# Last block of a block-FFT convolution: products in place over the x spectra, one summing visit per third

## The chip, the cores and the metric

The kernel runs on one NeuronCore of one Trainium2 chip. Its engines run their own instruction streams in program order and meet through semaphores: TensorE (PE, matmuls into PSUM), VectorE (DVE), ScalarE (ACT), GpSimd (POOL) and SyncE (SP, which here only issues DMAs). The metric is the device time of one execution in microseconds (us); less is better. Kernels are compared by the median of several executions on the same chip.

## The reference

The output is the concatenation of two independent halves of 576 channels each, over S = 2048 positions. Half A is a sliding attention with 32 heads of 18 channels, a window of 8 positions at dilation 2, and two projections. Half B is a gated long convolution:

```python
def _B_ref(q, k, v, shift_k, ssm_k, ssm_D):
    ...
        k_shift = k_shift + k_pad[:, t:t + S, :] * shift_k[:, ks - 1 - t][None, None, :]
    kv = k_shift * v
    ...
    y_f = kv_f * kf_f[None, :, :, :]
    y = irfft(y_f)[:S]
    y = y + kv * ssm_D[None, None, :]
    return q * y
```

The change lies wholly in half B. What is computed is not altered by it.

## The kernel before

**The convolution by blocks.** The 2048 positions are cut into NBL = 4 blocks of 512. For each block i the spectrum of kv is made once and kept in the SBUF tile `xw` at `HB * XG[i]`, in three parts of HB = 2304 columns: two components and their sum. The filter's four block spectra lie in the tile `Ks` in the same manner. The spectrum of output block j is the sum over i = 0..j of (x spectrum i) times (filter spectrum j - i). The three parts let one complex product be made with three real ones. Each part's columns are worked on in three thirds t of QTR = 768 columns (192 channels by four frequency groups).

**Products (L1092 to L1101).** `products(j, t, i)` is one VectorE multiply of 128x2304 (three parts of 768 columns) of `xw` by `Ks`. The result goes to one of five homes: places in the tiles `av`, `v`, `qk` (two) and `Ks` that are free by then. Block 3 rotates over the first four of them, block 2 over all five. There are 30 products in the list `todo` (L1225), in the order j, t, i: numbers 0 to 2 for block 0, 3 to 8 for block 1, 9 to 17 for block 2, and 18 to 29 for block 3 (18 to 21 are third 0 with i = 0 to 3, 22 to 25 third 1, 26 to 29 third 2).

**Sums (L1105 to L1141).** `sums` adds a group of products into two PSUM accumulators `ps_z` (r = 0 and r = 1) by matmuls with plus or minus identity. TensorE works as four 64x64 tiles there, and one product is 16 matmuls, shown in the trace as four rows of four. After the last product of a third (i = j), ScalarE evicts r = 0 and then r = 1 to `av` (L1139); only the very last r = 1 goes over VectorE (L1137).

**The inverse transform (L1146 to L1222).** It is cut into units that TensorE does between the sums. For blocks 0 to 2 the 576 channels go in two halves a and b, each with three units, queued in the order a0, b0, a1, b1, a2, b2. Units 0 and 1 are eight 128x128 matmuls each (L1158) into the same PSUM tile: unit 0 starts it, ScalarE copies the result out (L1161), unit 1 accumulates on top of it, and ScalarE copies again. Unit 2 (`back`) is eight 64x64 matmuls (L1199) on the copies, evicted by ScalarE at L1206. Unit a0 or a1 needs only thirds 0 and 1 of its block, b0 or b1 thirds 1 and 2. Two such PSUM tiles (tag A) exist, so a and b have one each. Block 3 is different: after its third 1, units u0 and u1 (128x384) and a `back` are queued for the first 384 channels; the last 192 channels go through `last` (L1171) at the very end. After `back` of half b comes the gate: one VectorE multiply by q (L1212), three stores from SP (L1080, L1083) and, for blocks 0 and 1, the load of a later q by three DMAs on POOL (L1087, L1089).

**What sets the order.** The program's order is each engine's order. `groups` (L1229 to L1234) says which products are summed in one visit of TensorE. Block 0 has one product to a visit, block 1 two, block 2 three. Block 3 has pairs, and its last product, 29, is a visit of its own: 18,19 / 20,21 / 22,23 / 24,25 / 26,27 / 28 / 29. Ahead of a visit `sums` calls `until()` once, or twice for a group of more than two; each call takes the next number from the tuple `PLACES` (L19) and puts that many queued units ahead of the visit. The last seven numbers are 1, 2, 1, 4, 1, 1, 0. So the order on TensorE from the end of block 2's sums is: a0, sums 18 19, b0 a1, sums 20 21, b1, sums 22 23, a2 b2 (the queue is then empty), sums 24 25, u0, sums 26 27, u1, sums 28, sums 29, `back`, `last`.

The loop at L1253 emits products ahead of the visit that uses them, up to two past the group's last one, and one fewer at the group that ends with product 17 (L1254). Gates that are due are emitted ahead of the next product (L1242); the gate of block 2 is kept back until after product 29 (L1249).

Of the kernel before, what the change touches and what calls it, by code (L numbers as in the profile page):

```python
# [39 lines left out]
def view(t, offset, dims):  # L40

    return bass.AP(tensor=t.tensor, offset=t.offset + offset, ap=[list(t.ap[0])] + [list(d) for d in dims])
# [3 lines left out]
def kernel(  # L46
# [37 lines left out]
    NBL, BL = 4, 512  # L84
# [4 lines left out]
    HB = 4 * D  # L89
    QTR = 768  # L90
# [21 lines left out]
    xw = main.tile([128, 12 * HB], BF16, name="xw")  # L112
# [5 lines left out]
    XG = (9, 0, 3, 6)  # L118
# [52 lines left out]
    def k_at(m, part):  # L171
        return 3 * HB * (3 - m) + HB * part
# [139 lines left out]
    def dve(n, fn, ready=0.0, ns=0.53):  # L312

        fn()
        clk["D"] = max(clk["D"], ready) + n * ns / 1000 + 0.125
        return clk["D"]
# [23 lines left out]
    def need(label):  # L340
        while any(u[2] == label for u in units):
            pop()
# [369 lines left out]
    for i in range(NBL):  # L712
# [30 lines left out]
        for n, u in enumerate(mirrors):  # L743
            n = AT[n] if n < 2 else AT[i]
# [347 lines left out]
    def products(j, t, i):  # L1092

        homes = ((av, 0), (v, 6912), (qk, 9216), (qk, 9216 + HB), (Ks, k_at(3, 2)))
        n = npr[0]
        pr = view(*homes[(4, 1, 2, 3, 0)[(n - 9) % 5] if j == 2 else n % 4 if n < 9 else (n - 18) % 4], [[QTR, 3], [1, QTR]])
        npr[0] += 1
        r = dve(3 * QTR, lambda: nc.vector.tensor_tensor(  # L1098
            pr, view(xw, HB * XG[i] + QTR * t, [[HB, 3], [1, QTR]]),
            view(Ks, k_at(j - i, 0) + QTR * t, [[HB, 3], [1, QTR]]), ALU.mult))  # L1100
        return pr, r  # L1101
# [3 lines left out]
    def sums(j, t, group):  # L1105

        for _ in range(1 + (len(group) > 2)):
            until()
        for i, pr, ready in group:
            out = sum_of(j, t, i, pr, ready)  # L1110
        return out
# [113 lines left out]
    todo = [(j, t, i) for j in range(NBL) for t in range(3) for i in range(j + 1)]  # L1225
# [2 lines left out]
    clk["P"] = clk["D"]  # L1228
    groups = []  # L1229
    for n, (j, t, i) in enumerate(todo):  # L1230
        if (i if j == 2 else i % 2) and (j, t, i) != todo[-1]:
            groups[-1].append(n)
        else:
            groups.append([n])  # L1234
    prs, made_to = {}, 0

    def produce(n):
        if n < len(todo):
            j, t, last = todo[n]
            for i in range(last + 1):  # L1240
                need(f"fx{i}")
            due(1.0)  # L1242
            for new, tile_, at in ((last == 0, Ks, k_at(j, 0)), (last == j, xw, HB * XG[j])):
                if new and (j == 0 or t == 0) and (tile_ is xw, at) not in given:
                    at, w = (at + QTR * t, QTR) if j == 0 else (at, HB)
                    a, b, c = (view(tile_, at + HB * part, [[1, w]]) for part in range(3))
                    dve(w, lambda: nc.vector.tensor_tensor(c, a, b, ALU.add))
            prs[n] = products(*todo[n])
            if n == len(todo) - 1:  # L1249
                while late:  # L1250
                    late.popleft()[1]()

    for group in groups:  # L1253
        while made_to < min(group[-1] + 3 - (group[-1] == 17), len(todo)):  # L1254
            produce(made_to)
            made_to += 1
        j, t, i = todo[group[-1]]
        if (t, todo[group[0]][2]) == (0, 0):
            need(f"inv{j - 2}")
        r = sums(j, t, [(todo[n][2],) + prs.pop(n) for n in group])  # L1260
        new = []
        if i == j and t == 2 and j < NBL - 1:
            a, b = inverse(j, 0, HD, r), inverse(j, HD, HD, r)
            new = [a[0], b[0], a[1], b[1], a[2], b[2]]
        elif i == j and j == NBL - 1 and t > 0:
            new = inverse(j, 0, 2 * TH, r) if t == 1 else inverse(j, 2 * TH, TH, r)
        for u in new:
            units.insert(sum(w[2][:3] == "inv" for w in units), u)
# [35 lines left out]
```

## Time and profile before

| | |
|---|---|
| median of 3 runs | 214.94 us (214.34 to 215.21) |
| the profiled execution | 215.25 us |
| its span in the profile | 213.5 us |
| share of the chain that ended last | PE 51%, DVE 23%, DMA 9%, ACT 7%, issue 6% |
| granted TensorE clock over the span | 0.998 |

In the timeline, a row is a run of like instructions of one engine: its start and its duration in us, the engine, the line of the kernel, the operation, output and input, and how many. In brackets stands the idle time before it on its engine, and what ended that idle time. The rows of one engine can overlap a little, since its instructions are pipelined; start to start is then the better measure. Ahead of the stretch that the change touches lie the projections, the attention and the forward spectra (to about 152 us of the span); block 3's own sums run from 190.5 us to 205.9 us, and the end of the kernel is the inverse of block 3's last 192 channels, its gate and its stores.

### The profile page before, as it was taken

Reading aid. Unit: us, or ns where it says so; the run is one execution under the profiler, and the core shown is the slowest. Engines: PE = TensorE matmul, PEld = TensorE weight load, DVE = VectorE, ACT = ScalarE, POOL = GpSimd, SP = SyncE. Lnnn points to the kernel's source line nnn. Section 1 sums busy time; section 2 is a strip of 40 time slices with the busy share of each in tenths; the row PEclk is TensorE's granted clock in tenths of the full one; section 3 lists DMA queues with packets and bytes.
Section 4 is the critical chain, followed back from the end, with each engine's and each line's share of the span. In section 5 each row is a group of like instructions: output and inputs, shape, how many; then the busy total and the mean of one; then the engine's idle time right before and its main releaser. Section 6 shows DMA issues by size and latency. Waiting matters only on the chain.

```text
span 213.5 us, 5089 instructions
## 1 busy us (share of the span) xinstructions
PE 200.7 (94%) x2114; PEld 112.0 (52%) x2122; DVE 197.6 (93%) x150; ACT 150.8 (71%) x218; POOL 68.6 (32%) x104
## 2 busy tenths in 40 slices
PE   7999899999879999999999999998999999999891
PEld 3443344445545656453355456765566667666560
DVE  7989999999969999979999999979999999799972
ACT  4699764787897979975378568964578797756630
POOL 8999992102683255220190000004330001102000
PEclk9999999999999999999999999999999999999999
DMA  6999999999492655998999893957994105353033
GB/s 209 295 325 228 275 323 298 229 144 223 91 140 27 86 71 98 187 164 179 225 249 220 173 228 87 167 182 174 235 251 138 60 3 166 114 169 111 3 110 111
DMA packets 34084, 36.12 MB, mean 169 GB/s; under 512 B 17459, under 2 KB 28847, under 8 KB 34062
## 3 DMA queue, kind: packets, MB, share of 16 engines
q1 hardware_dynamic: 26380, 23.11, 44.7%
q0 software_dynamic: 5216, 10.19, 25.3%
q10 hardware_dynamic: 2466, 2.51, 3.4%
q8 instruction: 16, 0.26, 0.5%
q14 instruction: 6, 0.05, 0.1%
HBM read 13.11 MB, written 4.72 MB: 83 GB/s over the span
## 4 chain that ended last, share of the span: by engine, by line
PE 51%; DVE 23%; DMA 9%; ACT 7%; issue 6%; SPq 2%; DVEq 0%; ACTq 0%
DVE tB L560 9%; PE ps_z L1126 9%; DVE xw L564 8%; PE ps_inv L1158 7%; PE ps_wo L1020 6%; PE ps_proj L363 5%; PE ps_acc L964 4%; PE ps_fk L610 4%; PE ps_fx L766 4%; DMA TB<-av 4%; PE ps_log L837 3%; DMA xw<-in_A_wqkv_dram 3%; DMA kj<-in_B_k_dram 2%; DVE av L947 2%; ACT Ks L670 2%
## 5 line engine op out<-in xcount | busy, mean ns | idle before, releaser
L363 PE MATMUL ps_proj<-xw 128*128 128x512 bf16 x153 | 36.6, 380 | 1.3 <-issue 0.6
L822 DVE TENSOR_TENSOR av<-qk 128x4096 bf16<-128x4096 bf16 (+1 forms) x16 | 31.5, 2018 | 2.3 <-ACT xw L592 2.1
L363 PEld LDWEIGHTS <-xw 128*128 128x128 bf16 x160 | 14.3, 98 | 20.6 <-issue 5.9
L1098 DVE TENSOR_TENSOR qk<-xw,Ks 128x2304 bf16<-128x2304 bf16 x14 | 18.7, 1355 | 2.0 <-PE ps_z L1126 1.7
L1139 ACT ACTIVATE av<-ps_z 128x768 bf16<-128x768 f32 x23 | 17.4, 809 | 4.3 <-PE ps_z L1126 4.3
L397 ACT ACTIVATE qk<-ps_proj 128x1024 bf16<-128x1024 f32 x14 | 14.3, 1023 | 8.4 <-PE ps_proj L374 4.5
L768 ACT ACTIVATE xw<-ps_fx 128x576 bf16<-128x576 f32 x32 | 18.7, 669 | 1.1 <-PE ps_fx L766 1.1
L560 DVE TENSOR_TENSOR tB<-kj,skb 128x4608 bf16<-128x4608 bf16 (+1 forms) x8 | 19.3, 2416 | 0.1
L670 ACT ACTIVATE Ks<-ps_fk 128x576 bf16<-128x576 f32 x32 | 18.6, 687 | 1.2 <-PE ps_fk L611 1.2
L766 PE MATMUL ps_fx<-xw,TB 128*128 128x288 bf16 x128 | 18.0, 286 | 0.9 <-ACT xw L592 0.7
L1020 PE MATMUL ps_wo<-qk 128*128 128x288 bf16 x128 | 17.6, 287 | 0.0
L610 PE MATMUL ps_fk<-Ks,TB 128*128 128x384 bf16 x62 | 16.5, 326 | 1.0 <-ACT Ks L670 0.7
L964 PE MATMUL ps_acc<-av,ident 64*64 64x512 bf16 x160 | 15.7, 378 | 0.7 <-DVE av L947 0.7
L1158 PE MATMUL ps_inv<-av,TI 128*128 128x288 bf16 (+1 forms) x112 | 15.7, 292 | 0.6 <-ACT av L1139 0.6
L766 PEld LDWEIGHTS <-TB 128*128 128x128 bf16 x128 | 11.8, 97 | 7.3 <-issue 4.6
L397 ACT ACTIVATE v<-ps_proj 128x1024 bf16<-128x1024 f32 x9 | 9.4, 1039 | 8.8 <-PE ps_proj L374 4.5
L611 PE MATMUL ps_fk<-Ks,TB 128*128 128x192 bf16 x62 | 15.2, 245 | 0.0
L1087 POOL DMA_DIRECT2D TB<-in_B_q_dram x4 | 3.0, 738 | 37.8 <-DVE v L1098 23.8
L968 ACT ACTIVATE qk<-ps_acc 128x1024 bf16<-128x1024 f32 x8 | 8.2, 1024 | 9.7 <-PE ps_acc L964 9.7
L1020 PEld LDWEIGHTS <-qk 128*128 128x128 bf16 x128 | 11.7, 98 | 5.3 <-issue 2.5
L947 DVE TENSOR_TENSOR av<-Ks,v 128x4096 bf16<-128x4096 bf16 x6 | 13.7, 2286 | 0.8 <-PE ps_acc L964 0.8
L1161 ACT ACTIVATE v<-ps_inv 128x576 bf16<-128x576 f32 (+1 forms) x14 | 9.5, 677 | 6.4 <-PE ps_inv L1158 6.3
(194 smaller groups left out, 467.6 us busy)
## 6 DMA issues: line engine op xcount, KB each, us to landing
Ks<-Ks POOLq DMA_DIRECT2D x7, 576.0 KB, 8.7
TB<-av SPq DMA_DIRECT2D x12, 256.0 KB, 5.4
kj<-in_B_k_dram SPq DMA_DIRECT2D x6, 504.0 KB, 6.0
vt<-in_B_v_dram SPq DMA_DIRECT2D x8, 288.0 KB, 4.9
Ks<-av SPq DMA_DIRECT2D x8, 256.0 KB, 5.4
out_dram<-qk ACTq DMA_DIRECT2D x5, 288.0 KB, 4.0
Ks<-in_A_x_dram SPq DMA_DIRECT2D x2, 576.0 KB, 5.2
xw<-in_A_wqkv_dram SPq DMA_DIRECT2D x2, 576.0 KB, 5.9
```

The source lines that it names most:

```text
L363: nc.tensor.matmul(ps[:, jp, :], wq(kb, comp, 128 * ct, 128), xT(kb, 1024 * jj + 512 * jp, 512), **se)
L397: nc.scalar.activation(view(t, o + pad + 1024 * jj, [[512, 2], [1, 512]]), ps[:], ACT.Copy)
L560: dve(2304 * n, lambda: nc.vector.tensor_tensor(to, view(kj, row * D, [[D, n], [D, 4], [1, D]]), view(skb, row * D, [[D, n], [0, 4], [1, D ...
L610: nc.tensor.matmul(o[:, 0:2], w, rhs[:, 0:2], start=start, stop=stop)
L670: nc.scalar.activation(view(Ks, k_at(m, cs ^ (m & 1)) + 96 * gi, [[768, 3], [384, 2], [1, 96]]), acc3(ps), ACT.Copy, scale=(PSG, MSG)[cs][ ...
L766: nc.tensor.matmul(ps[:, pm, 0:HD], TX[:, 2 * pm + c, 128 * gi:128 * gi + 128], kv[:, 2 * c + pm, HD * h:HD * h + HD], start=(c == 0), sto ...
L768: nc.scalar.activation(view(xw, HB * XG[i] + 96 * gi + 1152 * h, [[HB, 2], [384, 3], [1, 96]]), view(ps, 0, [[512, 2], [96, 3], [1, 96]]), ...
L822: return P, at, step, dve(1024 * nj, lambda: nc.vector.tensor_tensor(view(P, at, [[step, 4], [256, nj], [1, 256]]), view(t, o + 256 * hh, ...
L964: nc.tensor.matmul(acc[64 * o:64 * o + 64, h, :], ident[64 * h:64 * h + 64, 64 * h:64 * h + 64], view(P, 256 * u, [[2048, 2], [1, 256]])[6 ...
L1020: nc.tensor.matmul(ps[:, r, 0:HD], oT(hh, j + 2 * r, t)[:, o:o + 128], wo[:, t // 2, t % 2, HD * h:HD * h + HD], start=(t == 0 and h == 0) ...
L1126: nc.tensor.matmul(view(acc[r], 512 * h, [[192, 2], [96, 2], [1, 96]])[o:o + 64], w[64 * h:64 * h + 64, 64 * h:64 * h + 64], pr[64 * h:64 ...
L1158: nc.tensor.matmul(ps[:, c, 0:n], TI[:, sl, pm, 128 * c:128 * c + 128], Yall[:, j % 2, pm, sl, c0:c0 + n], start=(pm == 0 and sl == 0), st ...
```

## The change

Three places are edited. Products of block 3 are written over the x spectrum that they are made from (each product of block 3 is the last reader of its slice of `xw`), so they use none of the homes. In `groups`, a visit of block 3 now holds a whole third, other than the very last product: 18 to 21, 22 to 25, 26 to 28, and 29. And the exception for the group that ends with product 17 is gone, so that products 18 and 19 are both emitted ahead of that group's sums. `PLACES` is as it was. Blocks 0 to 2 keep their homes and groups.

```diff
@@ products
         homes = ((av, 0), (v, 6912), (qk, 9216), (qk, 9216 + HB), (Ks, k_at(3, 2)))
         n = npr[0]
-        pr = view(*homes[(4, 1, 2, 3, 0)[(n - 9) % 5] if j == 2 else n % 4 if n < 9 else (n - 18) % 4], [[QTR, 3], [1, QTR]])
+        pr = view(*homes[(4, 1, 2, 3, 0)[(n - 9) % 5] if j == 2 else n % 4], [[QTR, 3], [1, QTR]]) if j < NBL - 1 else \
+            view(xw, HB * XG[i] + QTR * t, [[HB, 3], [1, QTR]])
         npr[0] += 1
@@ groups
-        if (i if j == 2 else i % 2) and (j, t, i) != todo[-1]:
+        if i and (j, t, i) != todo[-1]:
             groups[-1].append(n)
         else:
             groups.append([n])
@@ the loop over groups
-        while made_to < min(group[-1] + 3 - (group[-1] == 17), len(todo)):
+        while made_to < min(group[-1] + 3, len(todo)):
             produce(made_to)
             made_to += 1
```

## The prediction

> **What bounds it now.** First the page, for which engines are full:
>
> ```profile
> PE 200.7 (94%) x2114; PEld 112.0 (52%) x2122; DVE 197.6 (93%) x150; ACT 150.8 (71%) x218; POOL 68.6 (32%) x104
> ```
>
> TensorE and VectorE are both nearly full, so the averages decide nothing; what counts is which of them ends last where the change is. Next the chain of waits (start, length, engine, what), in the stretch of block 3:
>
> ```profile
> 198.31 1.19 ACT v L1206 x2
> 199.50 0.02 issue
> 199.52 0.82 ACT av L1139
> 200.34 0.04 issue
> 200.38 1.46 PE ps_inv L1158 x8
> 201.84 1.42 PE ps_z L1126 x32
> 203.27 1.41 PE ps_inv L1158 x8
> 204.67 1.45 PE ps_z L1126 x32
> ```
>
> The chain is TensorE's own work, with one stop at 199.5 to 200.4, where u0 waits for ScalarE to evict the sums of third 1. An eviction's end releases TensorE 0.04 us later (200.34 to 200.38). VectorE is not in it. Third, the timeline of TensorE, cut to the points where the kind of work changes:
>
> ```profile
> 189.16 0.33 PE L1126 MATMUL ps_z<-qk,identn 64*64 64x384 bf16 x4
> 189.43 1.15 PE L1158 MATMUL ps_inv<-av,TI 128*128 128x288 bf16 x8
> 190.51 0.36 PE L1126 MATMUL ps_z<-av,ident 64*64 64x384 bf16 x4
> 190.70 0.49 PE L1126 MATMUL ps_z<-av,identn 64*64 64x384 bf16 x8
> ...
> 191.94 2.13 PE L1158 MATMUL ps_inv<-av,TI 128*128 128x288 bf16 x16
> 194.00 0.36 PE L1126 MATMUL ps_z<-qk,identn 64*64 64x384 bf16 x4
> ...
> 200.38 1.46 PE L1158 MATMUL ps_inv<-av,TI 128*128 128x384 bf16 x8 [0.59 <-ACT av L1139]
> 201.77 0.36 PE L1126 MATMUL ps_z<-av,ident 64*64 64x384 bf16 x4
> ...
> 205.93 0.33 PE L1199 MATMUL ps_back<-v,flip 64*64 64x384 bf16 x4
> ```
>
> Every inverse unit before stands alone or beside a unit of the other half, with sums after it. And the timelines of ScalarE and VectorE:
>
> ```profile
> 190.62 0.66 ACT L1161 ACTIVATE v<-ps_inv 128x576 bf16<-128x576 f32 x1
> ...
> 196.62 0.66 ACT L1161 ACTIVATE v<-ps_inv 128x576 bf16<-128x576 f32 x1
> ...
> 201.88 0.81 ACT L1161 ACTIVATE v<-ps_inv 128x768 bf16<-128x768 f32 x1 [0.85 <-PE ps_inv L1158]
> ```
> ```profile
> 182.94 1.36 DVE L1098 TENSOR_TENSOR qk<-xw,Ks 128x2304 bf16<-128x2304 bf16 x1 [1.52 <-PE ps_z L1126]
> 186.91 1.35 DVE L1212 TENSOR_TENSOR TB<-v,TB 128x2304 bf16<-128x2304 bf16 x1
> ...
> 201.13 2.62 DVE L1098 TENSOR_TENSOR qk<-xw,Ks 128x2304 bf16<-128x2304 bf16 x2
> ```
>
> VectorE's last long wait for a home to come free is at 182.94. That is product 17, of block 2. From there to 203.75 it runs without a stop, so no product of block 3 waits for a home.
>
> **Part 1, products in place.** Nothing is removed that costs time: the same twelve multiplies, and no wait of block 3 to take away. The price of a multiply over its own input is not shown for L1098. The nearest rows are the gate, which overwrites its input (1.352 us at L1212), the in-place adds at L564 (1.358 us) and the products themselves (1.354 us). So it lies between -0.02 and +0.05 us over twelve products; I take 0. It would be hidden in any case: product 21 ends at 193.6, 25 at 198.7 and 29 at 203.75, while the order below wants them at 194.4, 199.3 and 206.4. Without that cover (0.6 us at the tightest) a delay of VectorE would go straight to the end.
>
> **Part 2, product 19 ahead of block 2's last sums.** On VectorE it changes places with the gate of block 1 (186.91), which comes one product later (1.27 us, start to start). Three stores on SP and three loads of q on POOL (191.81) move with the gate. Nothing else is queued on SP until 205.05 or on POOL to the end, and that q is first used at 207.02, some 12 us after the moved loads are issued (191.81 to 193.73 before, 1.3 later now). Cost 0.
>
> **Part 3, visits by thirds.** The calls of `until` come to the same seven, two of them now ahead of each large group. With 1, 2, 1, 4, 1, 1, 0 the order becomes: a0 b0 a1, sums 18 to 21, b1 a2 b2, sums 22 to 25, u0 u1, sums 26 to 28, sums 29, `back`, `last`. All matmuls are the same; what differs between 189.43 and 205.93 is switches and waits.
>
> *Switches.* A row of four of the sums takes 0.16 us; after the one at 189.16 the 128-wide unit starts at 189.43, not 189.32: 0.11. Eight matmuls of 128 take 1.08 us to the next start (189.43 to 190.51), sixteen 2.06: so eight cost 0.98 and the switch back 0.10, and the first row of four after it takes 0.19, not 0.16: 0.13. Before there are nine switches, five of them back; after, five, three of them back. Saved: 2 x 0.11 + 2 x 0.13 = 0.48 us.
>
> *a1 behind b0.* a1 accumulates onto the PSUM tile that a0's eviction reads. b0 (0.98) covers it: a0's eviction ends at 190.62 + 0.66 = 191.28, and a1 is up at 189.43 + 2 x 0.98 = 191.39. Cost 0, with 0.07 to spare after the 0.04 of release; without b0 between it would be 0.9.
>
> *b2 behind b1.* b2 needs b1's eviction, which sums 22 and 23 cover today. If b1 starts at s, its eviction starts at s + 1.19 (195.43 to 196.62), takes 0.66 and releases at s + 1.89. TensorE is free at s + 0.98 + 0.13 + 0.24 (a2, two rows of four at 0.12) = s + 1.35. New wait 0.54 us. Behind it in TensorE's queue stand all sums of third 1, and so their eviction and u0.
>
> *u1 behind u0.* u1 accumulates onto the tile of u0, and sums 26 and 27 cover u0's eviction today. That one ends at 201.88 + 0.81 = 202.69 and releases at 202.73; u0's issue ends at 201.77 less the 0.10 of the switch, 201.67. New wait 1.06 us. Behind it are the sums of third 2, hence ScalarE's and VectorE's last evictions, `back` and `last`: the end.
>
> *u0's wait* for the sums of third 1 (199.62 to 200.38) stays: the accumulators are released by the last rows of a visit, however long it is, and ScalarE is free by then, with b2's eviction two microseconds back.
>
> The trace of before holds no pair of units on one tile back to back, so the two waits are bounded: at the low end none, at the high end the lengths just worked out; I take the high ends, since the chain's row at 200.38 has TensorE waiting for a ScalarE eviction just so. The Trainium skill, PSUM — Partial Sum Buffer, section Terms, speaks against the change here: TensorE writing a bank while ScalarE reads the same bank and quadrant is an error, so the wait between u0 and u1 can't be left out. By that rule the sum is the one below; were overlap allowed, 1.06 less.
>
> **Sum:** -0.48 + 0.54 + 1.06 = +1.12 us. All behind 205.93 moves along unchanged (7.6 us to the end of the span). The span goes from 213.5 to 214.6, the profiled run from 215.25 to 216.4; that run lies 0.3 above the median shown, 214.94, which goes to 216.06, say **216.1 us**. That is 0.5%, which is also about what a measurement of this kernel can tell from no change (1.07 us): the forecast stands on the line.
>
> **Rivals.** *The other side: only the switches count.* If the evictions of b1 and u0 are out of TensorE's way, 0.48 us is gained: 214.5. For it: four units of block 1 in a row (177.76, 4.09 us for 32 matmuls) show no wait at all. Against: a and b alternate there, and each unit covers the other's eviction; u0 has no partner. It decides once the two waits together come under 0.48.
> *Only u1 waits*, because ScalarE gets b1 out in a2's time: -0.48 + 1.06 = +0.58, 215.5. Against: the 0.66 of the eviction is longer than a2's 0.24.
> *VectorE was the bound*, and homes that need not come free give back its waits for TensorE, 1.52 and 0.19 us (182.94 and 173.71): 213.2. Against: both are products of block 2, whose homes stay.
> *A false conflict in `xw`.* If reads of one third count as overlapping with writes of the next, since the slices interleave, sums 18 and 19 wait for products 22 and 23 (done at 194.9 and 196.1 in place of 192.5 and 193.1 needed): +3.0 there, 0.2 more at sums 23 (product 27 ends at 201.2), and the +1.12 of the waits and switches: +4.3, some 219; without those, 218. Against: a0 starts at 189.43 on columns of `av` that interleave with those that the eviction of 189.22 is still writing.
>
> **How the numbers follow.** Forecast 0.64, with its own range 215.7 to 216.5; only u1 0.17; switches alone 0.08; false conflict 0.07; VectorE 0.04. The range 215.1 to 217.2 holds the forecast and most of the second case, and above it the scatter of the runs (0.4 either way) on a wait that is longer than worked out. Slower by over 0.5%: some five in seven of the forecast and the false conflict, 0.53. Within 0.5%: the rest of the forecast and two rivals, 0.43. Faster: 0.04.
>
> **What would show it.** Right: TensorE idle about 0.5 us ahead of the second `back` near 197 and about 1.1 us ahead of u1 near 202, both put down to L1161; the sums of third 1 near 197.3 to 199.9 and of third 2 near 204.4 to 207.1; five switches; VectorE's last product still ending near 203.75 and at 1.35 us a multiply. Wrong: no idle time ahead of u1, products longer than 1.40 us, or sums that wait for a product.

## The result, and the profile after

The changed kernel is slower: median 216.42 us of ten runs against 214.68 of ten runs of the kernel before, ratio 1.0061 with a 95% interval of 1.0032 to 1.0090. Some executions are some per cent longer than the rest (three of the ten after, 220.25 to 221.30 us): the ratios leave such executions out, the medians don't, and the profile of "thirds, old homes" below is of one. The fastest runs are 215.50 and 214.34, so 1.16 us apart. The forecast was +1.12 us, 216.1 us in a range of 215.1 to 217.2.

The spans of the two profiled executions say less: 213.8 us after, 213.5 before. The reason stands far ahead of the change, in the timeline of VectorE; first the kernel before, then the changed one:

```profile
143.23 2.29 DVE L947 TENSOR_TENSOR qk<-TB,v 128x4096 bf16<-128x4096 bf16 x1 [0.80 <-DMA TB<-av]
```
```profile
142.35 2.29 DVE L947 TENSOR_TENSOR qk<-TB,v 128x4096 bf16<-128x4096 bf16 x1
```

In the profiled execution of before, VectorE stood idle for 0.80 us until a broadcast of attention weights had landed; in that of after it did not wait. Both kernels run the same instructions there. So two spans can't be compared, and two things are compared below. One is **the stretch**: from the start of unit a0 to the start of block 3's `back`, within which all of the change lies. It is 205.93 - 189.43 = 16.50 us before and 206.22 - 188.54 = 17.68 us after, 1.18 more. The other is the fastest run, in which such delays should be smallest.

The page's first part after, where only VectorE's and TensorE's lines moved, and those hardly:

```profile
PE 200.6 (94%) x2114; PEld 112.8 (53%) x2122; DVE 197.4 (92%) x150; ACT 150.8 (71%) x218; POOL 68.6 (32%) x104
```

The chain of waits after (start, length, what):

```profile
194.10 1.51 ACT av L1140 x2
195.62 0.55 ACT v L1162
196.17 0.04 issue
196.21 0.44 PE ps_back L1200 x8
196.65 2.31 PE ps_z L1127 x54
198.96 0.02 issue
198.98 0.82 ACT av L1140
199.80 0.04 issue
199.84 1.48 PE ps_inv L1159 x8
201.32 0.02 issue
201.34 0.82 ACT v L1162
202.16 0.04 issue
202.20 1.46 PE ps_inv L1159 x8
203.66 2.75 PE ps_z L1127 x64
```

Lines of the changed kernel are one higher than before (L1162 is the unit's eviction, L1140 that of the sums). Before, ScalarE stood in the chain once in this stretch, ahead of u0. Now it stands there three times: ahead of b2 (196.21), ahead of u0 (199.84) and ahead of u1 (202.20). Ahead of b2 the chain goes through the two evictions of third 0's sums to that of b1; b1's own matmuls end just then too (194.31 + 1.16 = 195.47, and its eviction starts at 195.50), so either alone would have put that eviction there. The timeline of TensorE has the same three places:

```profile
188.54 3.12 PE L1159 MATMUL ps_inv<-av,TI 128*128 128x288 bf16 x24
...
194.31 1.16 PE L1159 MATMUL ps_inv<-av,TI 128*128 128x288 bf16 x8
195.39 0.32 PE L1200 MATMUL ps_back<-v,flip 64*64 64x288 bf16 x4
195.54 0.29 PE L1200 MATMUL ps_back<-v,flipn 64*64 64x288 bf16 x4
196.21 0.32 PE L1200 MATMUL ps_back<-v,flip 64*64 64x288 bf16 x4 [0.38 <-ACT v L1162]
...
199.84 1.46 PE L1159 MATMUL ps_inv<-av,TI 128*128 128x384 bf16 x8 [0.59 <-ACT av L1140]
202.20 1.46 PE L1159 MATMUL ps_inv<-av,TI 128*128 128x384 bf16 x8 [0.90 <-ACT v L1162]
203.59 0.36 PE L1127 MATMUL ps_z<-xw,ident 64*64 64x384 bf16 x4
...
206.22 0.33 PE L1200 MATMUL ps_back<-v,flip 64*64 64x384 bf16 x4
```

The idle times in brackets count from the modelled end of the last matmul, which overlaps the next one's start when nothing waits. Start to start is what the wait costs: a2's second row would have let b2 start at 195.54 + 0.12 = 195.66, so b2 lost 0.55 us; u1 could have started at 199.84 + 1.29 = 201.13 (a 128x384 unit's matmuls take 1.29 us, 1.39 to the sums less the switch of 0.10), so it lost 1.07. The 24 matmuls of a0, b0 and a1 run without a gap.

VectorE after: two products of block 2, each with the wait for a home that it had before, and products 21 to 29 in one row:

```profile
172.83 1.36 DVE L1099 TENSOR_TENSOR qk<-xw,Ks 128x2304 bf16<-128x2304 bf16 x1 [0.19 <-PE ps_z L1127]
...
182.05 1.36 DVE L1099 TENSOR_TENSOR qk<-xw,Ks 128x2304 bf16<-128x2304 bf16 x1 [1.52 <-PE ps_z L1127]
...
191.21 11.51 DVE L1099 TENSOR_TENSOR xw<-xw,Ks 128x2304 bf16<-128x2304 bf16 x9
```

Nine multiplies without a stop, 1.27 us from start to start, and done at 202.7; each is ready before the sums that use it, product 25 by the least, some 0.8 us.

### The profile page after: what moved, and what is told of

It is laid out like the page before. It is cut to its first block, busy times and chain, and to the rows that moved or that the text cites. A ratio compares the mean times of both kernels' runs of the same rounds, so it can differ in the third digit from the quotient of the medians.

```text
span 213.8 us, 5083 instructions
## 1 busy us (share of the span) xinstructions
PE 200.6 (94%) x2114; PEld 112.8 (53%) x2122; DVE 197.4 (92%) x150; ACT 150.8 (71%) x218; POOL 68.6 (32%) x104
## 4 chain that ended last, share of the span: by engine, by line
PE 60%; DVE 20%; ACT 8%; DMA 5%; issue 5%; SPq 1%; DVEq 0%; ACTq 0%
DVE tB L560 9%; PE ps_z L1127 9%; PE ps_fx L766 8%; DVE xw L564 8%; PE ps_wo L1020 7%; PE ps_acc L964 7%; PE ps_inv L1159 7%; PE ps_proj L363 5%; PE ps_fk L610 4%; PE ps_log L837 3%; DMA xw<-in_A_wqkv_dram 3%; DMA kj<-in_B_k_dram 2%; ACT Ks L670 2%; ACT av L1140 2%; DVE av L822 2%
## 5 line engine op out<-in xcount | busy, mean ns | idle before, releaser
L1140 ACT ACTIVATE av<-ps_z 128x768 bf16<-128x768 f32 x23 | 17.4, 809 | 8.5 <-PE ps_z L1127 8.5
L1099 DVE TENSOR_TENSOR xw<-xw,Ks 128x2304 bf16<-128x2304 bf16 x12 | 15.5, 1351 | 0.1
L1159 PEld LDWEIGHTS <-TI 128*128 128x128 bf16 x112 | 10.5, 98 | 6.5 <-issue 3.5
```

Source lines behind the costliest of these rows:

```text
L1140: nc.scalar.activation(y, z, ACT.Copy)
L1159: nc.tensor.matmul(ps[:, c, 0:n], TI[:, sl, pm, 128 * c:128 * c + 128], Yall[:, j % 2, pm, sl, c0:c0 + n], start=(pm == 0 and sl == 0), st ...
```

## The experiments

All ran beside the kernel before, whose fastest run was 214.32 to 214.34 in every comparison. The table has the stretch (from one profiled execution of each), its difference to that of before (16.50), the difference of the fastest runs, and the ratio.

| kernel | stretch, us | to before | fastest run | ratio (95% interval) |
|---|---|---|---|---|
| changed, again | 17.68 | +1.18 | +1.18 | 1.0062 (1.0025 to 1.0099) |
| in place, old visits | 16.50 | 0.00 | +0.01 | 1.0001 (0.9974 to 1.0029) |
| thirds, old homes | 17.67 | +1.17 | +1.18 | 1.0035 (1.0008 to 1.0061) |
| thirds 0 and 1 merged | 16.85 | +0.35 | +0.35 | 1.0000 (0.9973 to 1.0027) |
| third 2 merged | 17.33 | +0.83 | +0.84 | 1.0033 (1.0006 to 1.0059) |
| u1 on its own tile | 16.62 | +0.12 | +0.14 | 1.0011 (0.9981 to 1.0041) |
| b1 early | 17.53 | +1.03 | +1.05 | 1.0040 (1.0009 to 1.0071) |
| other work behind each eviction | 17.38 | +0.88 | +0.88 | 1.0032 (1.0005 to 1.0059) |
| third 0 merged | 16.27 | -0.23 | -0.22 | 0.9996 (0.9960 to 1.0031) |

The intervals are some 0.3% either way. Delays like the one at 143.23, which several of the profiles show ahead of the stretch, are the likely reason; for the runs without a profile that is not shown. The stretch and the fastest run agree within 0.02 us in every row, and the verdicts rest on these two.

**The changed kernel again.**

> The changed kernel as it is, as an anchor beside the others. Measure: the stretch from the start of unit a0 to the start of block 3's back, 16.50 us before and 17.68 us in the first profile of the changed kernel. Expected again 17.7 us, with TensorE idle some 0.5 us ahead of b2 and some 1.1 us ahead of u1; ratio to before 1.005.

The stretch is 17.68 us to the hundredth (191.09 to 208.77), with the same 0.38 and 0.90 of idle time, though this execution came to the stretch 2.6 us later than the first.

**In place alone.** Edit to the changed kernel:

```diff
-        if i and (j, t, i) != todo[-1]:
+        if (i if j == 2 else i % 2) and (j, t, i) != todo[-1]:
```

> Products in place and product 19 emitted early, but block 3 summed in the visits of before (pairs). Theory (all of the loss is in the merged visits): stretch 16.5 us, ratio 1.000. Rival (writing over the input, or moving product 19 ahead of the gate, costs VectorE something): product longer than 1.36 us or the stretch above 16.8 us.

No difference at all. The groups of VectorE in the profile (by shape; busy us, mean ns, then idle us) have both kinds of product in one execution, over the input and into the home `qk`:

```profile
L1099 DVE TENSOR_TENSOR xw<-xw,Ks 128x2304 bf16<-128x2304 bf16 x12 | 15.5, 1352 | 0.1
L1099 DVE TENSOR_TENSOR qk<-xw,Ks 128x2304 bf16<-128x2304 bf16 x8 | 10.8, 1355 | 1.9 <-PE ps_z L1127 1.7
```

Writing over the input costs nothing, and the 1.7 us of waiting for a home is still there, since it belongs to block 2. So in place is neither the loss nor a gain.

**Thirds without in place.** Edit to the kernel before; block 3's products are emitted only as far as the visit needs, since four homes hold no more:

```diff
-        if (i if j == 2 else i % 2) and (j, t, i) != todo[-1]:
+        if i and (j, t, i) != todo[-1]:
...
-        while made_to < min(group[-1] + 3 - (group[-1] == 17), len(todo)):
+        while made_to < min(group[-1] + (1 if group[0] > 17 else 3 - (group[-1] == 17)), len(todo)):
```

> Thirds in one visit, but products in the old four homes, each emitted no further ahead than its visit needs. Theory (in place buys nothing, the order on TensorE is all): stretch 17.7 us as in the changed kernel, and VectorE never idle by more than 0.2 us ahead of a product of block 3. Rival (a home that comes free late holds the products back, and in place is what makes the visits by thirds bearable): VectorE idle ahead of products 22 to 29, stretch 18.2 us or more.

The stretch is the changed kernel's (195.44 to 213.11). The profiled execution reached it late, after longer waits ahead of it (2.61 us at 65.27 for a DMA, 3.98 at 72.89 for the attention's sums), but within the stretch the granted clock was 1.00 and the waits are the same 0.38, 0.59 and 0.90. VectorE runs products 18 to 29 with no idle time ahead of any. The order on TensorE is all of the loss; the merged visits would not even have needed the products in place.

**The two halves of the merge.** Edits to the changed kernel, the first for thirds 0 and 1 alone, the second for third 2 alone:

```diff
-        if i and (j, t, i) != todo[-1]:
+        if (i % 2 if (j, t) == (NBL - 1, 2) else i) and (j, t, i) != todo[-1]:
```
```diff
-        if i and (j, t, i) != todo[-1]:
+        if (i % 2 if j == NBL - 1 and t < 2 else i) and (j, t, i) != todo[-1]:
```

> As the changed kernel, but third 2 summed in the visits of before (26 27, 28, 29), so that u1 comes after sums 26 and 27 and not right behind u0. Theory (u1 waits 1.07 us for the eviction of u0, which two sums cover; two switches of 0.24 us come back): stretch 17.68 - 1.07 + 0.24 = 16.85 us, no idle time ahead of u1. Rival (the wait ahead of u1 is not for u0's eviction, but ScalarE or the sums are late anyway): idle time only moves, stretch 17.7 us or above.

> The other half: thirds 0 and 1 in pairs as before, only third 2 merged (26 to 28 after u0 and u1). Theory: the wait ahead of u1 is there in full, b2's is not: 16.50 + 1.07 - 0.24 = 17.3 us for the stretch. If the parts add, this and the kernel with only thirds 0 and 1 merged lose 0.83 and 0.35 us against before, and the whole change 1.18.

Both came out to the hundredth: +0.35 and +0.83, which add up to the 1.18 of the whole. With sums 26 and 27 back between u0 and u1, nothing waits ahead of u1 (timeline of TensorE, thirds 0 and 1 merged):

```profile
200.28 1.46 PE L1159 MATMUL ps_inv<-av,TI 128*128 128x384 bf16 x8 [0.59 <-ACT av L1140]
201.67 0.36 PE L1127 MATMUL ps_z<-xw,ident 64*64 64x384 bf16 x4
...
203.10 1.47 PE L1159 MATMUL ps_inv<-av,TI 128*128 128x384 bf16 x8
```

**What u1 waits for.** Edit to the changed kernel:

```diff
-            if pm == 0:
+            own = j == NBL - 1 and pm == 1
+            if pm == 0 or own:
                 box["ps"] = bank2("ps_inv", "A")
...
-                                     Yall[:, j % 2, pm, sl, c0:c0 + n], start=(pm == 0 and sl == 0), stop=(sl == 3),
+                                     Yall[:, j % 2, pm, sl, c0:c0 + n], start=((pm == 0 or own) and sl == 0), stop=(sl == 3),
```

> As the changed kernel, but u1 of block 3 writes a PSUM tile of its own in place of accumulating on u0's (so the first 384 channels of block 3 lack the even part in one half: that part of the computation is left out). Theory (u1 waits because it shares the tile that ScalarE is reading): no idle time ahead of u1, stretch 17.68 - 1.07 = 16.6 us. Rival (u1 waits for something else: its operands or the evicted sums): idle time stays, stretch 17.7 us.

The two units run as one row of sixteen, and the stretch is 1.06 us shorter than the changed kernel's:

```profile
201.36 2.76 PE L1160 MATMUL ps_inv<-av,TI 128*128 128x384 bf16 x16 [0.59 <-ACT av L1140]
204.05 0.36 PE L1127 MATMUL ps_z<-xw,ident 64*64 64x384 bf16 x4
```

So u1's operands were there, and the wait is for the tile that ScalarE is still reading.

**A wait in place of a wait.** Edit to the changed kernel, in `PLACES` (its last seven numbers):

```diff
-    1, 2, 1, 4, 1, 1, 0,
+    1, 3, 1, 4, 1, 1, 0,
```

> As the changed kernel, with b1 moved ahead of the sums of third 0 (a0 b0 a1 b1, sums 18 to 21, a2 b2, sums 22 to 25). b2's wait for b1's eviction is then gone. Simple account: 0.55 us of waiting and 0.24 of switches go, stretch 16.9 us. Theory (a wait takes its place: only a2 and b2, 0.48 us, then lie between the sums of third 0 and those of third 1, which need the two accumulators evicted 0.75 and 1.44 us after the last sum): stretch 17.5 us, TensorE waiting for L1140 ahead of sums 22.

The stretch is 17.53, as the theory had it; the simple account had 16.9. b2's wait is gone, and TensorE waits ahead of and within sums 22 instead:

```profile
195.82 0.29 PE L1200 MATMUL ps_back<-v,flipn 64*64 64x288 bf16 x4
196.22 0.36 PE L1127 MATMUL ps_z<-xw,ident 64*64 64x384 bf16 x4
196.38 0.36 PE L1127 MATMUL ps_z<-xw,identn 64*64 64x384 bf16 x4
196.92 0.36 PE L1127 MATMUL ps_z<-xw,identn 64*64 64x384 bf16 x4 [0.18 <-ACT av L1140]
```

Sums 22 start at 196.22, not 195.94 (0.12 behind the last row of `back`), when accumulator r = 0 has been evicted, and the rows for r = 1 at 196.92, not 196.54. The two delays are 0.28 and 0.38 us. So this merged third needed some 1.1 us of other work behind it (the 0.48 of a2 and b2 and the 0.66 lost) until its two accumulators were free. In the kernel before, b1 and its switches stand in that place, 1.19 us from the last row of the sums (195.32) to the next sums (196.51), and nothing waits.

**Other work behind each eviction: a miss.** Edits to the kernel with thirds 0 and 1 merged; the gate of block 2 is emitted ahead of the visit of product 29, which leaves its place on VectorE as it was:

```diff
-    1, 2, 1, 4, 1, 1, 0,
+    1, 2, 1, 0, 3, 1, 0,
...
-            if n == len(todo) - 1:
-                while late:
-                    late.popleft()[1]()
...
+        if group[-1] == len(todo) - 1:
+            while late:
+                late.popleft()[1]()
         r = sums(j, t, [(todo[n][2],) + prs.pop(n) for n in group])
```

> A version that keeps the products in place and thirds 0 and 1 merged, but has other work behind each eviction: a0 b0 a1, sums 18 to 21, b1, sums 22 to 25, a2 b2 u0, sums 26 27, u1, sums 28, sums 29; block 2's gate follows product 29 as before. Theory: no wait ahead of b2 (-0.55) or u1 (-1.07 and two switches, +0.24), and a2 and b2 fill 0.48 of u0's wait for the sums of third 1: stretch 17.68 - 1.86 = 15.8 us, 0.7 us less than before, ratio 0.997. Rival (waits only move along the queue): 16.5 us or more.

It was 17.38, not 15.8. The waits ahead of b2 and u1 are gone as expected, but the account had left out two things (timeline of TensorE, then of ScalarE):

```profile
197.79 0.36 PE L1127 MATMUL ps_z<-xw,ident 64*64 64x384 bf16 x4 [0.16 <-DVE xw L1099]
...
198.80 0.32 PE L1200 MATMUL ps_back<-v,flipn 64*64 64x288 bf16 x4
200.46 1.46 PE L1159 MATMUL ps_inv<-av,TI 128*128 128x384 bf16 x8 [1.34 <-ACT v L1207]
```
```profile
198.35 1.51 ACT L1140 ACTIVATE av<-ps_z 128x768 bf16<-128x768 f32 x2 [2.11 <-PE ps_z L1127]
199.75 1.20 ACT L1207 ACTIVATE v<-ps_back 128x576 bf16<-128x576 f32 x2
```

u0 needs a PSUM tile, and only two of its kind exist. a2 and b2, placed right ahead of it, hold both, and ScalarE evicts them only after the two accumulators of third 1 (198.35 to 199.86). a2's eviction is done at 199.75 + 0.65 = 200.40, and u0 starts at 200.46. With the accumulator r = 0 alone to wait for (198.35 + 0.81 = 199.16 and the 0.04 of release) it could have started at 199.20, so the tile cost 1.26. And product 25 is now wanted before it is ready: its sums start 0.33 us late (197.79, not 197.46). The two make 1.59, against the 1.56 by which the stretch is longer than the account's 15.82.

**The part of the merge that pays.** Edit to the changed kernel:

```diff
-        if i and (j, t, i) != todo[-1]:
+        if (i % 2 if j == NBL - 1 and t > 0 else i) and (j, t, i) != todo[-1]:
```

> Products in place, only third 0 merged (18 to 21 behind a0 b0 a1), thirds 1 and 2 in the visits of before. This merge leaves no unit right behind the eviction that it needs: a1 has b0 ahead of it, b1 alone (1.2 us) lies between the sums of third 0 and of third 1, and a2 b2 come after sums 22 and 23. Theory: only a pair of switches goes, stretch 16.50 - 0.24 = 16.26 us, fastest run 0.2 us below that of before, ratio 0.999. Rival (the merge itself costs, whatever it covers, because sums start later or product 25 is late): 16.5 us or more, with TensorE waiting for L1099 or L1140 ahead of sums 22 or 25.

The stretch is 16.27 us (190.97 to 207.24) and the fastest run 214.10, both 0.2 below the kernel before. The interval of the ratio holds 1, so the whole times alone don't show it; the stretch, with the same instructions in it, does. TensorE waits in it only ahead of u0, as before:

```profile
190.97 3.11 PE L1159 MATMUL ps_inv<-av,TI 128*128 128x288 bf16 x24
...
201.69 1.46 PE L1159 MATMUL ps_inv<-av,TI 128*128 128x384 bf16 x8 [0.59 <-ACT av L1140]
...
207.24 0.33 PE L1200 MATMUL ps_back<-v,flip 64*64 64x384 bf16 x4
```

## Why the prediction was right

**The total.** +1.12 us was forecast, +1.18 measured in the stretch and +1.16 and +1.18 in the fastest runs. That is on the line of 0.5%, as the prediction said; the ratio, 1.0061, lies just past it. What follows the stretch takes 7.6 us as before. That the forecast of 216.1 lies so near the median of 216.42 is in part luck: it was added to a median of three runs, 214.94, where that of ten is 214.68, and the medians of ten are 1.74 apart. What bears the prediction out is the change in the stretch and its terms.

**u1 behind u0** (1.06): 1.07 in the timeline, and 1.06 came back when u1 had a tile of its own. It was the largest term, and the mechanism named for it is shown: the tile, not the operands. The rule of the Trainium skill that the prediction names there (PSUM — Partial Sum Buffer, Terms: TensorE writing a bank and quadrant while ScalarE reads it is an error) agrees with this trace as far as the wait is there; what happens without a wait was not tried.

**b2 behind b1** (0.54): 0.55 in the timeline, and no wait in the kernels with other work between the two (third 2 merged, third 0 merged, b1 early).

**Switches** (-0.48 for two pairs): one pair is the whole difference of the kernel with only third 0 merged, -0.23 against -0.24. The other is what is left in the kernel with third 2 merged beside u1's wait, 0.83 - 1.07 = -0.24. The count of nine and five leaves out the switch into u0, which falls into u0's wait in both kernels; the timelines have ten and six.

**a1 behind b0** (0): no gap in the row of 24 matmuls, though only 0.07 us was to spare.

**u0's wait** (unchanged): 0.79 us, from 198.89 + 0.16 = 199.05 to 199.84, where it was 0.76. With the other three terms this makes 0.55 + 1.07 - 0.47 + 0.03 = 1.18.

**In place and the moved gate** (0): 0.00 in the kernel that has both without the merge. The sums of third 1 reach product 25 at 198.40, some 0.8 us after it is made (191.21 + 4 x 1.27 + 1.35 = 197.64). That this cover mattered was seen where it was missing, in the kernel with a2 and b2 moved.

**The rivals.** Switches alone (214.5) and u1 alone (215.5) fall with the two waits seen. VectorE as the bound falls with the changed kernel's own trace, where block 2's waits for homes, 0.19 and 1.52 us, are all still there, and with the kernel of in place alone, which gains nothing. A false conflict in `xw` falls with the row of nine products and with sums that wait for none.

**What was not foreseen** is how far the whole times scatter. The prediction took 0.4 us either way from three runs, while the ten runs after spread from 215.50 to 221.30, and to 217.72 without the three longest. Some profiles show waits for DMAs ahead of the change (0.80, 1.00 and 2.61 us); how much of the spread they make is not shown.

## What to carry to other kernels

Small visits of an engine can be what hides another engine's evictions. Before merging them, list for each unit what it waits for and what then stands between; in an engine that works in order, a switch saved (0.23 us a pair here) is soon paid back by one uncovered eviction (1.07). And when a unit is moved to cover a wait, count the PSUM tiles that it holds as well as its time: here the cover itself took the tile that the next unit needed.

## What the runs showed of the hardware

A VectorE multiply that overwrites one of its inputs takes as long as one into another tile (1352 and 1355 ns). TensorE goes on 0.04 to 0.06 us after the end of a ScalarE eviction that it waits for (200.40 to 200.46, and 0.04 in the chain's rows). Changing TensorE from the sums' 64x64 tiles to a 128x128 unit and back costs some 0.23 us (the stretch with one pair fewer). And waits for DMAs differ from one execution to the next: VectorE waited 1.0 us for rows ahead of L636 in the second profile of the changed kernel and not at all in the first. The delay of 0.80 us at 143.23 was not made up: it is still there as 0.89 where the stretch starts (189.43 and 188.54).
